# First MoE: the low part of the activations subtracted on VectorE instead of GpSimd

## The chip, the cores and the metric

The kernel runs on one core of a Trainium2 chip. The core has a matmul engine (TensorE, PE in the rows), three engines for elementwise work (VectorE or DVE, ScalarE or ACT, GpSimd or POOL) and an engine that only starts transfers (SyncE, SP). Each runs its own queue of instructions in order, and semaphores tie the queues together. The metric is device time of one execution in microseconds; before the change it is 1246.03 us (median of three runs, 1245.34 to 1246.07).

## What is computed

Attention over 4 batches, 12 heads, 448 positions and 64 columns a head (with an RMS norm on q and k), then two layers of experts over the 1792 tokens. The change is in the first of them, which is one dense expert:

```python
def _moe_ref(x, w_in, w_out):           # x 1792x768, w_in 768x2048, w_out 2048x768
    h = x @ w_in
    g = np.maximum(0.01 * h, h)
    return (g @ w_out).astype(np.float32)
```

The second layer routes each token to one of 8 experts by the largest logit, and so needs the first layer's output to nearly full float32 precision.

## The kernel before

**Products in three parts.** TensorE gets its operands rounded (`fp32r`). To keep the precision, each operand is kept as a high part (rounded copy, by ScalarE) and a low part (the operand less its high part), and each product is the sum of three matmuls: high x high, high x low, low x high. The helper `lo_of(engine, dst, src, hi)` issues the subtraction that makes a low part, as one `tensor_tensor` on the engine it is given. All low parts in the profile stand under its line, L63.

**The first MoE** goes through the 2048 inner columns in 16 blocks `f` of 128, two at a time (a group `G`), and through the four batches `b` of 448 tokens. A unit of `first(f, b)` adds 18 matmuls (6 blocks of the model's 768 columns, times 3; L627 to L629) in a PSUM bank `mo`. ScalarE makes `g` = 0.01 of it, VectorE the larger of the two, ScalarE the high part `gh`, and another engine the low part `gl` (L636; the line that changes). There is one buffer for `g` (so a unit's `g` cannot be made before the `gl` of the unit before), four for `gh` and for `gl`, two banks `mo`. A tile of `second(G, d, b)` is 6 matmuls (2 blocks times 3; L646 to L648) in a PSUM bank `mp` (two banks), which VectorE adds to `ysum` (L654; in the first group ScalarE copies, L652). A group has 8 units and 24 tiles.

**The weights** arrive as 8-byte numbers and are decoded on the way: each half of a block goes through ScalarE's `mag` (L580), five steps on VectorE (`top` L581 to L583, `pw` L585, `raw` L586) and an addition on GpSimd (L588). The buffers of `top`, `pw` and `mag` are single, so a half's first step waits for the addition of the half before. Then ScalarE makes the high part (`w0h` or `w1h`, L596) and GpSimd the low part (`w0l` or `w1l`), called a split here. There are three buffers for `raw` and three of each split weight.

**What sets the order.** The program is written unit by unit, but within the first MoE a scheduler places the instructions of each engine's queue by its own estimate of times. So a change of one instruction's engine changes the order on all engines from there on. DMAs of the weights are in SP's queue.

Of the kernel before, what the change touches and what calls it, by code (L numbers as in the profile page):

```python
# [20 lines left out]
def attention_moe_moe2(  # L21
# [15 lines left out]
    nc = tc.nc  # L37
# [24 lines left out]
    def lo_of(engine, dst, src, hi):  # L62
        engine.tensor_tensor(dst, src, hi.bitcast(F32), ALU.subtract)  # L63
# [87 lines left out]
    def xT_of(b, c):  # L151
        return [t[:, b % 2, c] for t in xT[b // 2]]
# [463 lines left out]
    class FirstMoe:  # L616
# [4 lines left out]
        def first(self, f, b):  # L621
            hi, lo = self.w.done[0, f]
            wh_, wl_ = hi.rearrange("p (c f) -> p c f", c=KD), lo.rearrange("p (c f) -> p c f", c=KD)
            ph = self.p1.tile([P, S], F32, name="mo", bufs=2)
            for c in range(KD):
                xh, xl = xT_of(b, c)
                nc.tensor.matmul(ph, wh_[:, c], xh, start=(c == 0), stop=False)  # L627
                nc.tensor.matmul(ph, wh_[:, c], xl, start=False, stop=False)  # L628
                nc.tensor.matmul(ph, wl_[:, c], xh, start=False, stop=(c == KD - 1))  # L629
            g = self.mw.tile([P, S], F32, name="g", bufs=1)  # L630
            gh = self.mw.tile([P, S], F32R, name="gh", bufs=2 * GF)
            gl = self.mw.tile([P, S], F32R, name="gl", bufs=2 * GF)
            nc.scalar.activation(g, ph, AF.Copy, scale=0.01)
            nc.vector.tensor_tensor(g, ph, g, ALU.max)  # L634
            nc.scalar.activation(gh, g, AF.Copy)  # L635
            lo_of(nc.gpsimd, gl, g, gh)  # L636
            self.gs[f, b] = (gh, gl)
            self.w.use(0, f)

# [472 lines left out]
```

## Time and profile before

| | before |
|---|---|
| median of the runs | 1246.03 us |
| the profiled execution | 1244.74 us, of which the trace spans 1242.7 |
| TensorE busy | 1161.2 us (93%) |
| VectorE busy | 761.7 us (61%) |
| ScalarE busy | 497.6 us (40%) |
| GpSimd busy | 529.5 us (43%) |
| `gl` on GpSimd | 64 instructions, 76.8 us |

The first MoE lies between about 366 and 880 us; attention before it, the second MoE after it. A row of the trace reads: start and duration in us, engine, line, operation, output and inputs, and in square brackets how long the engine stood idle just before and what ended that. `x2` merges two in a row. A VectorE instruction that is held up by another engine's use of the memory counts as busy all the while, so its duration in the row shows it.

### The profile page before, as it was taken

Reading aid. Unit: us, or ns where it says so; the run is one execution under the profiler, and the core shown is the slowest. Engines: PE = TensorE matmul, PEld = TensorE weight load, DVE = VectorE, ACT = ScalarE, POOL = GpSimd, SP = SyncE. Lnnn points to the kernel's source line nnn. Section 1 sums busy time; section 2 is a strip of 40 time slices with the busy share of each in tenths; the row PEclk is TensorE's granted clock in tenths of the full one; section 3 lists DMA queues with packets and bytes.
Section 4 is the critical chain, followed back from the end, with each engine's and each line's share of the span. In section 5 each row is a group of like instructions: output and inputs, shape, how many; then the busy total and the mean of one; then the engine's idle time right before and its main releaser. Section 6 shows DMA issues by size and latency. Waiting matters only on the chain.

```text
span 1242.7 us, 19106 instructions
## 1 busy us (share of the span) xinstructions
PE 1161.2 (93%) x6988; PEld 931.5 (75%) x6988; DVE 761.7 (61%) x1262; ACT 497.6 (40%) x791; POOL 529.5 (43%) x365
## 2 busy tenths in 40 slices
PE   4899999988999899999999999999799999999997
PEld 2455555544668778888888888978588988988986
DVE  6777888866527884757575754346646169315446
ACT  2566666645335421222222322123335257324444
POOL 1567767756445541525252523110325046213334
PEclk9899999989899999999999999999799999999999
DMA  5212222110102220111111110153366049413556
GB/s 147 59 47 64 72 70 73 49 29 29 46 15 76 77 78 23 55 48 53 50 53 49 53 51 1 49 175 96 79 249 246 17 169 358 176 47 109 181 202 224
DMA packets 68081, 116.28 MB, mean 94 GB/s; under 512 B 6780, under 2 KB 45948, under 8 KB 67968
## 3 DMA queue, kind: packets, MB, share of 16 engines
q1 hardware_dynamic: 64528, 103.87, 26.1%
q0 software_dynamic: 3120, 11.02, 2.6%
q8 instruction: 57, 0.93, 0.3%
q14 instruction: 56, 0.46, 0.1%
q10 hardware_dynamic: 320, 0.00, 0.0%
HBM read 106.61 MB, written 12.58 MB: 96 GB/s over the span
## 4 chain that ended last, share of the span: by engine, by line
PE 65%; DVE 16%; issue 7%; POOL 5%; ACT 3%; DMA 3%; ACTq 0%; DVEq 0%; POOLq 0%; SPq 0%
PE sc L298 6%; PE av L309 6%; PE mp L646 4%; PE mo L627 4%; PE mo L628 4%; PE mo L629 4%; PE mp L647 4%; PE mp L648 4%; PE ph L990 4%; PE ph L988 3%; PE ph L989 3%; DVE top L583 3%; PE py L1006 3%; PE py L1004 3%; PE py L1005 3%
## 5 line engine op out<-in xcount | busy, mean ns | idle before, releaser
L654 DVE TENSOR_TENSOR ysum<-mp,ysum 128x448 f32<-128x448 f32 x168 | 103.8, 621 | 113.0 <-PE mp L648 111.8
L313 POOL TENSOR_TENSOR pr<-pr,p 112x896 f32<-112x896 f32 x72 | 152.8, 2122 | 40.5 <-ACT p L300 26.5
L646 PE MATMUL mp<-gh,w1h 128*128 128x448 f32 x384 | 145.8, 381 | 19.9 <-DVE ysum L654 16.5
L627 PE MATMUL mo<-xTh,w0h 128*128 128x448 f32 x384 | 142.2, 370 | 7.0 <-DVE g L634 3.4
L647 PE MATMUL mp<-gl,w1h 128*128 128x448 f32 x384 | 142.4, 371 | 0.0
L628 PE MATMUL mo<-xTl,w0h 128*128 128x448 f32 x384 | 141.9, 369 | 0.2 <-DVE xTl L63 0.2
L629 PE MATMUL mo<-xTh,w0l 128*128 128x448 f32 x384 | 141.3, 368 | 0.0
L648 PE MATMUL mp<-gh,w1l 128*128 128x448 f32 x384 | 140.8, 370 | 0.0
L63 POOL TENSOR_TENSOR gl<-g,gh 128x448 fp32r<-128x448 f32 x64 | 76.8, 1201 | 139.9 <-ACT gh L635 113.2
L588 POOL TENSOR_TENSOR raw<-raw,top 128x384 f32<-128x384 f32 x64 | 64.7, 1012 | 139.2 <-DVE raw L586 114.8
L277 DVE TENSOR_REDUCE md<-tp 112x2 f32<-112x896 f32 x96 | 104.5, 1089 | 18.2 <-PE tp L275 18.0
L1004 PE MATMUL py<-w2h,hT 128*128 128x384 f32 x288 | 99.7, 346 | 0.0
L646 PEld LDWEIGHTS mp<-gh,w1h 128*128 128x128 f32 x384 | 72.8, 190 | 35.4 <-DVE ysum L654 13.8
L1006 PE MATMUL py<-w2l,hT 128*128 128x384 f32 x288 | 96.8, 336 | 0.0
L1005 PE MATMUL py<-w2h,hL 128*128 128x384 f32 x288 | 96.5, 335 | 0.0
L990 PE MATMUL ph<-w1l,xgh 128*128 128x512 f32 x216 | 86.3, 400 | 4.2 <-DVE w1l L63 4.2
L63 DVE TENSOR_TENSOR hL<-pt,hT 128x512 fp32r<-128x512 f32 x36 | 24.8, 689 | 106.2 <-ACTq L1014 59.3
L988 PE MATMUL ph<-w1h,xgh 128*128 128x512 f32 x216 | 86.8, 402 | 0.0
L989 PE MATMUL ph<-w1h,xgl 128*128 128x512 f32 x216 | 85.6, 396 | 0.0
L627 PEld LDWEIGHTS mo<-xTh,w0h 128*128 128x128 f32 x384 | 72.4, 189 | 15.9 <-DVE g L634 3.7
L580 ACT ACTIVATE mag<-wd 128x384 f32<-128x384 f32 x64 | 35.5, 555 | 118.5 <-DVE top L583 57.8
L63 POOL TENSOR_TENSOR w1l<-r,w1h 128x1024 fp32r<-128x1024 f32 x17 | 42.9, 2529 | 93.0 <-ACT w1h L952 75.1
(199 smaller groups left out, 2542.3 us busy)
## 6 DMA issues: line engine op xcount, KB each, us to landing
r<-in_moe_w_dram SPq DMA_DIRECT2D x27, 1024.0 KB, 6.5
r<-in_moe_w_dram SPq DMA_DIRECT2D x36, 768.0 KB, 7.3
wd<-in_moe_w_in_dram SPq DMA_DIRECT2D x32, 384.0 KB, 3.2
wd<-in_moe_w_out_dram SPq DMA_DIRECT2D x32, 384.0 KB
qk<-in_q_dram SPq DMA_DIRECT2D x24, 224.0 KB, 2.8
qk<-in_k_dram SPq DMA_DIRECT2D x24, 224.0 KB, 3.1
vv<-in_v_dram SPq DMA_DIRECT2D x24, 224.0 KB, 2.7
x2d<-xn SPq DMA_DIRECT2D x24, 224.0 KB, 2.9
```

Of the source, the lines that this page charges most:

```text
L63: engine.tensor_tensor(dst, src, hi.bitcast(F32), ALU.subtract)
L313: nc.gpsimd.tensor_tensor(st["pr"][:CP], st["pr"][:CP], p, ALU.add)
L627: nc.tensor.matmul(ph, wh_[:, c], xh, start=(c == 0), stop=False)
L628: nc.tensor.matmul(ph, wh_[:, c], xl, start=False, stop=False)
L629: nc.tensor.matmul(ph, wl_[:, c], xh, start=False, stop=(c == KD - 1))
L646: nc.tensor.matmul(py, hi[:, sl], gh, start=(j == 0), stop=False)
L647: nc.tensor.matmul(py, hi[:, sl], gl, start=False, stop=False)
L648: nc.tensor.matmul(py, lo[:, sl], gh, start=False, stop=(j == GF - 1))
L990: nc.tensor.matmul(ph[n], xh[:, c], w1l[:, c, s_], start=False, stop=(c == K1 - 1))
L1004: nc.tensor.matmul(py[n], hT[:, c], w2h[:, c, s_], start=(c == 0), stop=False)
L1005: nc.tensor.matmul(py[n], hL[:, c], w2h[:, c, s_], start=False, stop=False)
L1006: nc.tensor.matmul(py[n], hT[:, c], w2l[:, c, s_], start=False, stop=(c == K2 - 1))
```

## The change

One word: `gl` is made on VectorE.

```diff
@@ -633,7 +633,7 @@
             nc.scalar.activation(g, ph, AF.Copy, scale=0.01)
             nc.vector.tensor_tensor(g, ph, g, ALU.max)
             nc.scalar.activation(gh, g, AF.Copy)
-            lo_of(nc.gpsimd, gl, g, gh)
+            lo_of(nc.vector, gl, g, gh)
             self.gs[f, b] = (gh, gl)
             self.w.use(0, f)
```

The scheduler orders the queues anew. First, VectorE's queue at the start of a group of weights (the same rows come once in each group; `raw` is the step that waits for the split). Before:

```order
L654 TENSOR_TENSOR ysum<-mp,ysum 128x448 x3
L586 SCALAR_TENSOR_TENSOR raw<-wd,pw 128x384
L654 TENSOR_TENSOR ysum<-mp,ysum 128x448 x2
L634 TENSOR_TENSOR g<-mo,g 128x448
L654 TENSOR_TENSOR ysum<-mp,ysum 128x448 x2
```

After:

```order
L654 TENSOR_TENSOR ysum<-mp,ysum 128x448 x3
L63 TENSOR_TENSOR gl<-g,gh 128x448
L634 TENSOR_TENSOR g<-mo,g 128x448
L586 SCALAR_TENSOR_TENSOR raw<-wd,pw 128x384
L654 TENSOR_TENSOR ysum<-mp,ysum 128x448 x2
L63 TENSOR_TENSOR gl<-g,gh 128x448
L581 TENSOR_SCALAR top<-wd 128x384
```

`gl` and the `g` that depends on it now stand ahead of `raw`. Second, TensorE's queue at the same place, the end of the group's second `mp` tile (the waits are on VectorE and on GpSimd, by their semaphores). Before:

```order
L648 MATMUL mp<-gh,w1l 128x448 [waits Pool_49]
L648 MATMUL mp<-gh,w1l 128x448
L646 MATMUL mp<-gh,w1h 128x448 [waits DVE_49]
L647 MATMUL mp<-gl,w1h 128x448
L648 MATMUL mp<-gh,w1l 128x448
```

After:

```order
L648 MATMUL mp<-gh,w1l 128x448 [waits Pool_49]
L648 MATMUL mp<-gh,w1l 128x448
L627 MATMUL mo<-xTh_114,w0h 128x448 [waits DVE_49]
L628 MATMUL mo<-xTl_115,w0h 128x448
L629 MATMUL mo<-xTh_114,w0l 128x448
```

A whole unit of `mo` has moved ahead of the third tile. Further on in the group five `mp` tiles now follow each other in the midst of a decode. Third, VectorE's queue in that run of five tiles, after:

```order
L581 TENSOR_SCALAR top<-wd 128x384
L654 TENSOR_TENSOR ysum<-mp,ysum 128x448
L582 SCALAR_TENSOR_TENSOR top<-wd,top 128x384
L654 TENSOR_TENSOR ysum<-mp,ysum 128x448
L63 TENSOR_TENSOR gl<-g,gh 128x448
L583 SCALAR_TENSOR_TENSOR top<-mag,top 128x384
L654 TENSOR_TENSOR ysum<-mp,ysum 128x448
L585 TENSOR_SCALAR pw<-top 128x384
L634 TENSOR_TENSOR g<-mo,g 128x448
L654 TENSOR_TENSOR ysum<-mp,ysum 128x448
L586 SCALAR_TENSOR_TENSOR raw<-wd,pw 128x384
```

The decode's steps, a `gl` and a `g` now lie between the five tiles' `ysum`. Fourth, VectorE's queue at the start of the second group of weights (the stretch around 416 us before). Before:

```order
L586 SCALAR_TENSOR_TENSOR raw<-wd,pw 128x384
L581 TENSOR_SCALAR top<-wd 128x384
L634 TENSOR_TENSOR g<-mo,g 128x448
L582 SCALAR_TENSOR_TENSOR top<-wd,top 128x384
L583 SCALAR_TENSOR_TENSOR top<-mag,top 128x384
```

After:

```order
L586 SCALAR_TENSOR_TENSOR raw<-wd,pw 128x384
L634 TENSOR_TENSOR g<-mo,g 128x448
L63 TENSOR_TENSOR gl<-g,gh 128x448
L581 TENSOR_SCALAR top<-wd 128x384
L582 SCALAR_TENSOR_TENSOR top<-wd,top 128x384
```

This `g` has moved ahead of the decode's first step. GpSimd's queue keeps its splits and additions in the order they had in each group; only the rows of `gl` between them are gone.

## Rows read from the trace of the kernel before

**Rows 1.** The head of the page: span, busy time of each engine, instructions.
```profile
span 1242.7 us, 19106 instructions
PE 1161.2 (93%) x6988; PEld 931.5 (75%) x6988; DVE 761.7 (61%) x1262; ACT 497.6 (40%) x791; POOL 529.5 (43%) x365
```

**Rows 2.** Two stretches: length, then busy us of PE, PEld, DVE, ACT, POOL.
```profile
440.00:480.00 40.00, 35.63 (x165) 31.26 (x164) 30.67 (x51) 9.52 (x17) 14.45 (x12) 0.96 0.24 69
...
540.00:600.00 60.00, 57.40 (x279) 51.64 (x278) 39.76 (x69) 16.17 (x28) 24.68 (x20) 1.00 0.16 47
```

**Rows 3.** Groups of instructions: busy us, mean ns of one, idle before and releaser.
```profile
L654 DVE TENSOR_TENSOR ysum<-mp,ysum 128x448 f32<-128x448 f32 x168 | 103.8, 621 | 113.0 <-PE mp L648 111.8
...
L63 POOL TENSOR_TENSOR gl<-g,gh 128x448 fp32r<-128x448 f32 x64 | 76.8, 1201 | 139.9 <-ACT gh L635 113.2
```

**Rows 4.** Splits on VectorE in the second MoE: duration ns least/median/most.
```profile
L63 DVE TENSOR_TENSOR w1l<-r,w1h x31: 1216/1227/3436, 900.3 to 1216.4; 128x1024 fp32r<-128x1024 f32 x31
...
L63 DVE TENSOR_TENSOR w2l<-r,w2h x48: 942/946/2321, 905.4 to 1228.0; 128x768 fp32r<-128x768 f32 x48
```

**Rows 5.** Waits: who for whom, us in total, times, the longest.
```profile
ACT g L633 <- POOL gl L63: 59.7, 42, 2.6
...
PE mp L646 <- DVE ysum L654: 16.5, 13, 2.1
```

**Rows 6.** In order of time around 561 us (stall A), and its last repetition.
```profile
559.52 1.85 POOL L63 TENSOR_TENSOR w1l<-raw,w1h 128x768 fp32r<-128x768 f32 x1 [10.35 <-ACT w1h L596]
...
561.33 1.15 POOL L63 TENSOR_TENSOR gl<-g,gh 128x448 fp32r<-128x448 f32 x1
561.41 1.49 DVE L586 SCALAR_TENSOR_TENSOR raw<-wd,pw 128x384 f32<-128x384 uint32 x1 [1.35 <-POOL w1l L63]
...
561.49 0.60 PE L648 MATMUL mp<-gh,w1l 128*128 128x448 f32 x2
562.43 2.15 POOL L63 TENSOR_TENSOR w1l<-raw,w1h 128x768 fp32r<-128x768 f32 x1
...
563.48 0.47 PE L646 MATMUL mp<-gh,w1h 128*128 128x448 f32 x1 [1.39 <-DVE ysum L654]
...
750.43 0.47 PE L646 MATMUL mp<-gh,w1h 128*128 128x448 f32 x1 [1.39 <-DVE ysum L654]
```

**Rows 7.** In order of time from 584 to 592 us (stall B).
```profile
584.48 0.37 PE L627 MATMUL mo<-xTh,w0h 128*128 128x448 f32 x1
...
584.92 1.83 POOL L63 TENSOR_TENSOR w0l<-raw,w0h 128x768 fp32r<-128x768 f32 x1 [0.96 <-ACT w0h L596]
585.41 1.77 DVE L583 SCALAR_TENSOR_TENSOR top<-mag,top 128x384 f32<-128x384 f32 x1
...
589.70 0.36 DVE L581 TENSOR_SCALAR top<-wd 128x384 int32<-128x384 int32 x1 [1.12 <-POOL raw L588]
...
590.43 0.36 PE L629 MATMUL mo<-xTh,w0l 128*128 128x448 f32 x1
590.76 0.56 DVE L583 SCALAR_TENSOR_TENSOR top<-mag,top 128x384 f32<-128x384 f32 x1
591.23 0.62 DVE L654 TENSOR_TENSOR ysum<-mp,ysum 128x448 f32<-128x448 f32 x1
...
592.00 0.44 PE L646 MATMUL mp<-gh,w1h 128*128 128x448 f32 x1 [1.21 <-DVE ysum L654]
```

**Rows 8.** In order of time between 380 and 470 us, five rows.
```profile
382.19 1.51 DVE L583 SCALAR_TENSOR_TENSOR top<-mag,top 128x384 f32<-128x384 f32 x1
...
416.46 1.94 DVE L581 TENSOR_SCALAR top<-wd 128x384 int32<-128x384 int32 x1 [1.11 <-POOL raw L588]
416.50 0.54 ACT L633 ACTIVATE g<-mo 128x448 f32<-128x448 f32 x1
...
418.99 0.47 PE L627 MATMUL mo<-xTh,w0h 128*128 128x448 f32 x1 [3.36 <-DVE g L634]
...
465.24 1.29 DVE L581 TENSOR_SCALAR top<-wd 128x384 int32<-128x384 int32 x1 [0.64 <-POOL raw L588]
```

## Prediction

> **What bounds the kernel now.** I read the page's head first, then the stages, the stalls of the first MoE one by one, and last the queue orders of both kernels. TensorE is busy for 1161.2 of 1242.7 us, VectorE for 761.7, GpSimd for 529.5 [rows 1]: on average GpSimd, which the change relieves, is far from a bound. The average hides the stage, so the second view is the table of stretches: from 440 to 480 us TensorE works 35.63 of 40 us with VectorE at 30.67, from 540 to 600 us 57.40 of 60 with VectorE at 39.76 and GpSimd at 24.68 [rows 2]. What can be won is what TensorE waits, about a tenth in the first of these stretches and a twentieth in the second.
>
> The change touches 64 instructions of 1.20 us on GpSimd [rows 3]. They feed `gl`, and two things hang on them: the next `g`, since there is one buffer for it (ScalarE waited 59.7 us for `gl`, in 42 cases), and, through VectorE's queue, TensorE: it waits for `ysum`, which empties the two `mp` banks, 16.5 us in 13 cases [rows 5]. So I followed the waits for `ysum` in order of time. From 501 us on they repeat with each group of weights, every 62.3 us (563.48 to 750.43 is three periods): a wait of 1.39 us (stall A, at 563.48; five such in all) and one of 1.21 us (stall B, at 592.00; four in all) [rows 6, 7]. Matmuls start every 0.205 us (30 from 584.48 to 590.43 [rows 7]). So the one due after the pair that starts at 561.49 was due at 561.90, and A costs 563.48 - 561.90 = 1.58 us; B costs 592.00 - 590.64 = 1.36 us.
>
> What makes them: in A VectorE's `raw` waits until GpSimd's split `w1l` ends (559.52 + 1.85 = 561.37), and then takes 1.49 us, because `gl` runs on GpSimd from 561.33 to 562.48; `ysum` is queued behind it. In B the split `w0l` (584.92 to 586.75) holds `top` for 1.77 us, and `ysum`, queued behind the next decode's first step, comes at 591.23. The same steps of the decode with nothing beside them take 0.56 us (line 583) and 0.36 (line 581) [rows 7]; so these steps do not run while GpSimd works, and one that was waiting goes ahead of GpSimd's next operation: the `w1l` at 562.43 took 2.15 us where the one before took 1.85 [rows 6]. `gl`, with two inputs in SBUF like `raw`, I count as such a step; `ysum`, with one in PSUM, is not (mean 0.621 over 168 [rows 3]).
>
> **What the change costs and gives.** On GpSimd 64 x 1.20 = 76.8 us go; nothing waits less for that in itself, since splits and additions are released by ScalarE, TensorE and VectorE. On VectorE 64 subtractions come. No row shows this form there, so it is bounded: splits of two SBUF inputs take 0.942 us for 768 columns and 1.216 for 1024 at the least [rows 4], 1.07 ns a column, hence 0.942 - 320 x 0.00107 = 0.60 us for 448; `ysum`, of the same shape with one input in PSUM, takes 0.62 [rows 3]. From above, one that waits for a split: 0.60 + 1.85 = 2.45 us (the worst split on VectorE took 3.436 against 1.216, 2.2 us of waiting [rows 4]). From below, nothing at all where VectorE would have stood waiting anyway. I take 0.60 and count each collision where the order puts one. Behind a `gl` that waits for ScalarE's `gh` now stand `ysum`, `g` and the decode on VectorE; for them wait TensorE's `mp` and `mo` banks.
>
> *Start, 366 to 470 us.* Here the decode fills VectorE. In 11 places a decode step beside a `gl` takes 0.8 to 0.95 us longer (the first 1.51 instead of 0.56 at 382.19, the last 1.29 instead of 0.36 at 465.24 [rows 7, 8]): 11 x 0.86 = 9.4 us go. In the same stretch 12 subtractions of 0.60 come: 7.2 us. That leaves 2.2 us on a chain that TensorE sees here. The largest single wait, 3.36 us at 418.99, is for a `g` whose ScalarE half ended at 417.04 and which stood in the queue behind a `top` held by a split (416.46 + 1.94 = 418.40) [rows 8]; in the new order this `g` stands ahead of that `top`, and starts at about 417.1 instead of 418.33 (418.99 less one VectorE step of 0.62 and the handover): 1.2 us. Sum 3.4 us.
>
> *Steady part, stall A.* In the new order TensorE has a unit of `mo` (18 matmuls, 3.7 us) after the second `mp` tile, so `raw` and the `ysum` behind it have time. But this unit needs the bank that `g` frees, and VectorE's queue now reads `ysum` x3, `gl`, `g`, `raw`. `gl` waits for the split to end at 561.37, then 0.60 for itself, 0.54 for ScalarE's `g` [rows 8], 0.62 for VectorE's, and some 0.1 of handovers: 563.23. TensorE wanted to go on at 561.90: 1.33 us against 1.58 now, a gain of 0.25.
>
> *Steady part, stall B.* The old place is harmless in the new order, but TensorE now has five `mp` tiles in a row (30 matmuls, 6.15 us), just when the first `w0l` split runs: it is released by the last matmuls of the unit before. The split holds the decode step ahead of `ysum` for its 1.85 us; by counting steps the third tile of the run starts 1.4 us late and the fifth 0.3 more: 1.7 us against 1.36 now, a loss of some 0.3. Five times A and four times B cancel (-1.25 and +1.4): 0, +- 1 us.
>
> *Tail, from 780 us.* No decode is left, VectorE has room; the routing's chain at the end holds only one `gl`. Nothing, +- 1 us. DMAs keep their queue, SP's, and their places.
>
> Sum: 1244.74 us (the profiled execution) - 3.4 = 1241.3. The median of the runs, 1246.03, lies 1.3 above the profiled one; against it I expect 1242.6 us.
>
> The rule that speaks most against the change stands in the Trainium skill, "SBUF — State Buffer", section "Who interferes with whom": a VectorE instruction with two SBUF inputs collides with a GpSimd instruction that reads SBUF, and whichever issues first has the shared ports to its end. The 1.49 us beside `gl` agree [rows 6]; but of who is next when both wait the page says only that the order of issue decides, while the row of 2.15 us shows VectorE first. By the page alone GpSimd's second split could as well go first in A, which is the second rival below.
>
> **Rivals.**
> 1. *The gain at the start is hidden.* The decode is paced by its own loop (a decode step waits for the addition, as 1.12 us at 589.70 [rows 7]) and by the splits, which stay; then the 2.2 us are not seen and only the 1.2 us of one `g` are left, or not even these: 1245 us. For it: the largest excesses in rows 7 and 8, 1.2 to 1.6 us, belong to splits, not to `gl`. Against it: 11 places with `gl` in 90 us.
> 2. *Slower: in A the second split takes the port ahead of `gl`.* Its ScalarE half is ready in time, so GpSimd starts it at 561.37 and `gl` waits 1.85 us more, `g` and the whole `mo` unit with it: 3.2 us instead of 1.6, five times 1.6 = 8 us, less the 3.4 of the start: 1250.6 us. It decides when `gl` reaches VectorE's head after 561.37 (a late `gh`, behind two splits on ScalarE) or if the port is not given to the one who waits. Against it: the 2.15 us.
> 3. *Better than forecast.* The split in B comes a step later than I count and falls beside `ysum`, which it does not hold, or into the next `mo` unit. B goes (1.36 x 4 = 5.4 us) and A keeps its 0.25 x 5 = 1.25: 1246.03 - 3.4 - 6.7 = 1236 us. It needs VectorE to be ahead of my count by about one step, 0.6 us.
> 4. *The change doesn't do what it says.* In the new order GpSimd has only splits and additions in this stage; excluded.
>
> **How the numbers follow.** Forecast 0.40 (1238 to 1246 by itself), rival 1 0.23, rival 2 0.22, rival 3 0.15. No change means within 0.2% (2.5 us), which is about what a measurement of this kernel can tell. The forecast is faster in three of four cases, else the same; rival 1 is the same in 0.18 and slower in 0.05; rival 2 slower in 0.20; rival 3 faster. Faster 0.30 + 0.15 = 0.45, same 0.30, slower 0.25. The range reaches from rival 3 to rival 2, a little more on each side: 1235 to 1252 us.
>
> **What would show it.** In the trace after: (1) `gl` on VectorE, 0.6 us at its least and up to 2.4; (2) the wait at the first `mo` unit after the start of a group of weights, released by `g`, about 1.3 us, in place of A's for `ysum`: 3 us there is rival 2; (3) one or two waits for `ysum` within a run of five `mp` tiles, 1.7 us together, beside a `w0l` split: none there is rival 3; (4) the wait near 419 us down from 3.36 to about 2.1; (5) no decode step between 366 and 470 us stretched by 0.8 to 0.95 us, only by splits and by additions. I am wrong if the period is not 62.3 +- 1 us, or if new waits for `g` stand where none is now, `gl` holding VectorE while `gh` is late.

## The result and the profile after

The changed kernel took 1231.39 us (median of four runs, 1230.19 to 1232.06) against 1245.76 us beside it: a ratio of 0.9884 (0.9868 to 0.9900), 14.4 us faster. Forecast were 1242.6 us in a range from 1235 to 1252: the direction is right, the gain is four times the forecast one (3.4 us).

The head of the page after, to be read against [rows 1]; columns as there:

```profile
span 1228.4 us, 19094 instructions
...
PE 1158.2 (94%) x6988; PEld 930.8 (76%) x6988; DVE 775.5 (63%) x1326; ACT 500.3 (41%) x791; POOL 456.4 (37%) x301
```

GpSimd lost 73.1 us, VectorE gained only 13.8, though 64 subtractions came to it. The stretches of [rows 2], after (the third number from the end is the share of TensorE's clock that was granted, then come the share of the DMA engines and GB/s):

```profile
440.00:480.00 40.00, 39.64 (x192) 35.46 (x191) 31.15 (x58) 11.00 (x19) 9.80 (x8) 1.00 0.21 59
...
540.00:600.00 60.00, 59.05 (x285) 53.04 (x285) 43.37 (x80) 16.46 (x28) 15.99 (x12) 1.00 0.19 53
```

TensorE works 4.0 us more of the first 40 us and 1.65 more of the later 60: it waits for almost nothing there. The first stretch also differs in the granted clock, 0.96 in [rows 2] and 1.00 here. Before, TensorE waited for `ysum` three times between 459 and 468 us (0.74, 2.11 and 1.52 us), and from 467.16 to 470.57 us the clock was at the lower of its two levels (0.50, that is 1.2 of 2.4 GHz). Two of these waits, and matmuls at the lower and again at the full clock, before:

```profile
464.75 0.44 PE L646 MATMUL mp<-gh,w1h 128*128 128x448 f32 x1 [2.11 <-DVE ysum L654]
...
467.72 0.74 PE L646 MATMUL mp<-gh,w1h 128*128 128x448 f32 x1 [1.52 <-DVE ysum L654]
...
468.63 0.58 PE L648 MATMUL mp<-gh,w1l 128*128 128x448 f32 x1
469.00 0.58 PE L646 MATMUL mp<-gh,w1h 128*128 128x448 f32 x1
...
470.95 0.36 PE L646 MATMUL mp<-gh,w1h 128*128 128x448 f32 x1
471.15 0.37 PE L647 MATMUL mp<-gl,w1h 128*128 128x448 f32 x1
```

Matmuls start every 0.375 us there, and every 0.205 us at the full clock. In the changed kernel the waits are gone, and so is this stretch.

Rows of instructions after, for [rows 3]; then the durations of `gl` (least/median/most); then ScalarE's waits, for [rows 5]:

```profile
L654 DVE TENSOR_TENSOR ysum<-mp,ysum 128x448 f32<-128x448 f32 x168 | 103.8, 621 | 111.1 <-PE mp L648 109.5
...
L646 PE MATMUL mp<-gh,w1h 128*128 128x448 f32 x384 | 144.4, 377 | 1.4 <-ACT ysum L652 0.7
```

```profile
L63 DVE TENSOR_TENSOR gl<-g,gh x64: 607/617/1904, 330.5 to 849.0; 128x448 fp32r<-128x448 f32 x64
```

```profile
ACT g L633 <- DVE gl L63: 55.6, 44, 2.0
```

`ysum` is as long as before. TensorE's 16.5 us of waits for it are gone: all idle time ahead of these `mp` matmuls is 1.4 us; ScalarE waits for `gl` about as long as before, on another engine.

Where the 14.4 us came from is read by the first matmul of each group of `mp` tiles, after less before, on the two profiled executions (1152 such matmuls in each, in their order): -0.8 us at the first group, -3.9 at the second, -9.3 at the third, then about -1.5 a group to -15.2 at the seventh and -15.7 at the eighth; 1.5 us are given back from there to the end of the span. So some 8.5 us belong to the first two groups, and the steady period fell from 62.3 to 60.8 us (552.13 to 612.99 below is 60.86).

In the first two groups (128.9 us long before, 120.4 after) TensorE's idle time fell from 11.2 to 5.2 us: waits for VectorE's `ysum` from 4.4 to 0, for ScalarE's copy (L652) from 3.4 to 0.7, for `g` up from 3.4 to 4.1. Of its matmuls there 26 started at the lower clock before and 18 after, which by the two spacings above is 8 x 0.17 = 1.4 us. The remaining 1.2 us I did not place.

The start of a steady group after, the place of stall A [rows 6]; in order of time:

```profile
548.51 4.00 POOL L63 TENSOR_TENSOR w1l<-raw,w1h 128x768 fp32r<-128x768 f32 x2 [16.81 <-ACT w1h L596]
...
548.95 1.89 DVE L63 TENSOR_TENSOR gl<-g,gh 128x448 fp32r<-128x448 f32 x1
...
550.68 0.57 PE L648 MATMUL mp<-gh,w1l 128*128 128x448 f32 x2
...
550.88 0.54 ACT L633 ACTIVATE g<-mo 128x448 f32<-128x448 f32 x1 [1.24 <-DVE gl L63]
...
551.46 0.62 DVE L634 TENSOR_TENSOR g<-mo,g 128x448 f32<-128x448 f32 x1 [0.61 <-ACT g L633]
552.00 0.94 DVE L586 SCALAR_TENSOR_TENSOR raw<-wd,pw 128x384 f32<-128x384 uint32 x1
...
552.13 0.47 PE L627 MATMUL mo<-xTh,w0h 128*128 128x448 f32 x1 [0.88 <-DVE g L634]
...
612.99 0.47 PE L627 MATMUL mo<-xTh,w0h 128*128 128x448 f32 x1 [0.89 <-DVE g L634]
```

This is the forecast chain: `gl` stands behind the first split, goes ahead of the second, then ScalarE's `g`, VectorE's `g`, TensorE. Ten microseconds on, the first `w0l` split, where a wait of 1.7 us was forecast (stall B's successor):

```profile
562.92 0.36 DVE L581 TENSOR_SCALAR top<-wd 128x384 int32<-128x384 int32 x1 [1.19 <-POOL raw L588]
...
562.99 1.99 POOL L63 TENSOR_TENSOR w0l<-raw,w0h 128x768 fp32r<-128x768 f32 x1
...
563.51 0.62 DVE L654 TENSOR_TENSOR ysum<-mp,ysum 128x448 f32<-128x448 f32 x1 [0.23 <-PE mp L648]
...
564.05 1.35 DVE L582 SCALAR_TENSOR_TENSOR top<-wd,top 128x384 int32<-128x384 int32 x1
...
565.33 0.61 DVE L654 TENSOR_TENSOR ysum<-mp,ysum 128x448 f32<-128x448 f32 x1
...
565.99 0.19 PEld L646 LDWEIGHTS mp<-gh,w1h 128*128 128x128 f32 x1 [0.42 <-DVE ysum L654]
```

The decode step `top` slipped in 0.07 us ahead of the split, `ysum` ran through beside it (its `mp` is in PSUM), and only the next decode step was held, until 565.40; what is left on TensorE is 0.42 us in the weight load; the matmul behind it starts 0.20 us late. And the end of the first group, the wait of [rows 8]:

```profile
411.20 1.91 POOL L63 TENSOR_TENSOR w1l<-raw,w1h 128x768 fp32r<-128x768 f32 x1 [0.74 <-ACT w1h L596]
...
411.50 0.54 ACT L633 ACTIVATE g<-mo 128x448 f32<-128x448 f32 x1
...
411.55 1.97 DVE L583 SCALAR_TENSOR_TENSOR top<-mag,top 128x384 f32<-128x384 f32 x1
...
414.43 0.62 DVE L634 TENSOR_TENSOR g<-mo,g 128x448 f32<-128x448 f32 x1
...
415.10 0.69 PE L627 MATMUL mo<-xTh,w0h 128*128 128x448 f32 x1 [4.08 <-DVE g L634]
```

This wait grew, from 3.36 to 4.08 us: `g` now stands behind the last three steps of a decode half, the first of them held by a split.

### The profile page after: what moved, and what is told of

Same layout as the page of the kernel before. It is cut to its first block, busy times and chain, and to the rows that moved or that the text cites. A ratio compares the mean times of both kernels' runs of the same rounds, so it can differ in the third digit from the quotient of the medians.

```text
span 1228.4 us, 19094 instructions
## 1 busy us (share of the span) xinstructions
PE 1158.2 (94%) x6988; PEld 930.8 (76%) x6988; DVE 775.5 (63%) x1326; ACT 500.3 (41%) x791; POOL 456.4 (37%) x301
## 4 chain that ended last, share of the span: by engine, by line
PE 77%; DVE 10%; issue 5%; ACT 3%; DMA 2%; POOL 2%; ACTq 0%; DVEq 0%; POOLq 0%; SPq 0%
PE mo L627 6%; PE mo L628 6%; PE mo L629 6%; PE sc L298 6%; PE av L309 6%; PE mp L646 6%; PE mp L647 5%; PE mp L648 5%; PE ph L990 4%; PE ph L989 3%; PE ph L988 3%; PE py L1006 3%; PE py L1004 3%; PE py L1005 3%; DVE w1l L63 2%
## 5 line engine op out<-in xcount | busy, mean ns | idle before, releaser
L277 DVE TENSOR_REDUCE md<-tp 112x2 f32<-112x896 f32 x96 | 104.4, 1088 | 17.7 <-PE tp L275 17.4
L627 PEld LDWEIGHTS mo<-xTh,w0h 128*128 128x128 f32 x384 | 72.5, 189 | 24.1 <-DVE g L634 12.1
L63 POOL TENSOR_TENSOR w1l<-raw,w1h 128x768 fp32r<-128x768 f32 x16 | 31.4, 1984 | 141.7 <-ACT w1h L596 141.7
L300 ACT ACTIVATE p<-sc 112x896 f32<-112x896 f32 x72 | 66.0, 917 | 39.8 <-PE sc L298 35.6
```

## The experiments

Four accounts were set against each other. **Port**: a VectorE step with its operands in SBUF stands while GpSimd reads SBUF, so GpSimd's `gl` cost time on VectorE. **Queue**: GpSimd's own time and the places in its queue were what the change freed. **Chain**: the way from `g` over `gl` to the next `g` became shorter. **Order**: the scheduler's new order alone did it. "Decode steps" are lines 581 to 586 on VectorE. Ratios are to the kernel before, run beside each.

**1. Give GpSimd reads back** (the results of the added work are not used):

```diff
             lo_of(nc.vector, gl, g, gh)
+            if f < NF - GF:
+                for t in (tab, stab):
+                    nc.gpsimd.tensor_tensor(t, gh[:NTAB, :P].bitcast(F32), gh[:NTAB, :P].bitcast(F32), ALU.subtract)
```

> The kernel after, with dummy work put back on GpSimd where gl was: in the 56 units of the first seven groups two subtractions of 112x128, which wait for gh, read it twice and write zeros into two small tables that hold zeros until the last group. The order of the other queues stays nearly as after (TensorE: 63 of 6582 instructions stand elsewhere, all in the steady part). About 0.48 us each by the slope of GpSimd's splits, 54 us in all against gl's 77. Theory P (while GpSimd reads SBUF, VectorE's decode steps stand still): two thirds of the gain is lost again, 1239 to 1243 us. Theory Q (gl delayed the additions and splits in GpSimd's queue): 1235 to 1238. Theory C (the shorter way from g over gl to the next g) and theory O (the new order of the queues alone): 1231 to 1233.

1238.58 us, ratio 0.9939 (0.9915 to 0.9963): nearly half of the gain is gone and the period is back at about 62.0 us. The time lies between the numbers of the port theory (from 1239) and of the queue theory (to 1238), and the interval holds both. The rows show little of the loss as a step held by a dummy. One place: a dummy now stands between the two `w1l` splits, so the second begins later and meets more of `raw`:

```profile
493.95 1.83 POOL L63 TENSOR_TENSOR w1l<-raw,w1h 128x768 fp32r<-128x768 f32 x1
...
494.53 1.67 DVE L586 SCALAR_TENSOR_TENSOR raw<-wd,pw 128x384 f32<-128x384 uint32 x1
```

In the changed kernel this second split had half a microsecond left when `raw` came (0.94 us); here it had 1.25 (1.67). But no wait of TensorE follows from it. The wait that grew comes from the order: 63 of the 6988 matmuls in the trace changed places, and the last `mo` matmul on a `w0l` buffer is one of them (experiment 3).

**2. The same with fills, which read nothing** (four `memset` of 112x128 a unit on GpSimd, nothing else changed).

> As e1_reads, but the dummy work reads nothing: four memsets of 112x128 a unit on GpSimd, behind no wait but their own queue; the order of the instructions on TensorE, VectorE and ScalarE is that of the kernel after, instruction for instruction. Theory P: 1231 to 1233, as the kernel after, since nothing is read. Theory Q: as far back as e1_reads, some 1235 to 1238. Theories C and O: 1231 to 1233.

1243.04 us, ratio 0.9977 (0.9967 to 0.9987), but it tells nothing of the port: with no input, the fills of both tiles all ran within the first 55 us of the program. One tile's:

```profile
L639 POOL MEMSET tab<- x112: 194/199/229, 2.6 to 50.7; 112x128 f32 x112
```

The first matmul behind the attention then came 12.87 us later (378.84 against 365.97), and the period stayed at 60.8 us. 44.5 us of GpSimd, put at the start of the program, cost 13.

**3. Fills tied to their unit** by a copy of one column on ScalarE.

```diff
+            if f < NF - GF:
+                nc.scalar.activation(tab[:, :1], gh[:NTAB, :1].bitcast(F32), AF.Copy)
+                for _ in range(5):
+                    nc.gpsimd.memset(tab, 0.0)
```

> The changed kernel plus, per unit of all groups but the last, five GpSimd fills of 112x128 that read nothing (199 ns each by the run before, so about 1.0 us a unit, as much of GpSimd's time as the two dummy subtractions took, 1.08 us), tied to the unit by a one-column ScalarE copy so that they stand in the first MoE. Port theory (GpSimd's reads of SBUF hold VectorE): no reads are added, so it stays near the changed kernel, 1231 to 1234 us, period 60.8 us. Queue theory (GpSimd's time itself is what was freed): as with the dummy subtractions, 1237 to 1240 us, period near 62.0 us.

1235.74 us, ratio 0.9917 (0.9900 to 0.9935): between the two theories, so neither number held. In order of time at the place of the new wait:

```profile
567.03 0.37 PE L629 MATMUL mo<-xTh,w0l 128*128 128x448 f32 x1
...
567.55 1.84 POOL L63 TENSOR_TENSOR w0l<-raw,w0h 128x768 fp32r<-128x768 f32 x1 [1.58 <-ACT tab L638]
...
567.93 1.94 DVE L63 TENSOR_TENSOR gl<-g,gh 128x448 fp32r<-128x448 f32 x1
...
569.32 0.73 POOL L640 MEMSET tab<- 112x128 f32 x3
...
569.79 0.54 DVE L583 SCALAR_TENSOR_TENSOR top<-mag,top 128x384 f32<-128x384 f32 x1
```

The fills hold nothing: `top` takes its 0.54 us beside them, and of 91 such VectorE steps beside nothing but fills none took over 0.11 us longer than unheld. What moved is the `w0l` split. It waits for the last `mo` matmul that reads its buffer, which the new order (93 of the 6988 matmuls changed places) puts behind two `mp` tiles: it ends at 567.40, 2.7 us after the rest of its unit (the row names ScalarE's copy, which ends at the same time). So the split catches `gl`, which takes 1.94 us, and TensorE has a new wait of 1.05 us a group; the period grows by 0.7 us, to 61.6. Experiment 1 has the same late matmul, and 0.97 us of the same wait, which is most of the 1.2 us by which its period grew. Neither run is a clean measure of the port. The Trainium skill, "SBUF — State Buffer", section "Who interferes with whom", says that a VectorE instruction with two SBUF inputs collides with a GpSimd instruction that reads SBUF and not with one that only writes; the last row here agrees.

**4. A written order**: the first MoE's loop issued in program order, once with `gl` on GpSimd, once on VectorE, with the same order on TensorE and ScalarE.

> The kernel before, but from the end of attention on the first MoE's queues are in the order in which the program is written, not the scheduler's; gl on GpSimd. The base for e8_manual_vector. It will be slower than before, since decode and units are not interleaved: 1260 to 1300 us by all theories.

> As e7_manual_gpsimd with gl on VectorE: TensorE's and ScalarE's queues have the same order in both, VectorE's has only the 64 subtractions more. Theories P and C: faster than e7_manual_gpsimd by 6 to 14 us, most of the gain without any new order. Theory O: within 3 us of e7_manual_gpsimd, or slower.

1455.41 us (1.1671, 1.1648 to 1.1695) and 1483.45 us (1.1895, 1.1871 to 1.1919): here the same move is 28 us **slower**, where both port and chain had it faster; the order account alone allowed that. The base missed its expectation too, by over 150 us: TensorE ran at the lower clock for 291 us in the one and 299 in the other, against 58 in the kernel before. What TensorE waits for in the two, `gl` on GpSimd first:

```profile
PE mp L646 <- DVE ysum L654: 128.3, 10, 14.0
```

```profile
PE mp L646 <- DVE ysum L654: 151.8, 26, 15.7
```

I read this as sums that stand at the end of VectorE's queue: 64 x 0.626 = 40 us more in the queue come out as 23.5 us more of wait for `ysum`, with all 6988 matmuls in the same order. So added VectorE work has a price, and it depends on what is queued behind it.

**5. The change for the first two groups alone, and for the others alone** (`nc.vector if f < 2 * GF else nc.gpsimd`, and the reverse).

> The low part of g on VectorE for the first two groups alone, on GpSimd after. If the gain is local to where the subtraction stands (port), the first 9.3 us of the 14.4 remain and the 1.5 us per period do not: about 1236.5 us, first stretch as in the changed kernel, period near 62.3 us. If the gain comes from one new order of the queues that spans the stage, the steady period could stay near 60.8 us and the time near 1231 us, or the whole gain go, 1243 us or more.

> The complement: GpSimd for the first two groups, VectorE after. Port theory: only the 1.5 us a period of the steady groups, some 4 to 6 us in all: about 1240 to 1242 us, with the stalls of 390, 411 and 459 to 468 us back. If the two halves don't add up (this run's gain and that of the first two groups together well under or over 14.4 us), the order of the queues has a part of its own.

1236.06 us (0.9926, 0.9906 to 0.9946) and 1241.09 us (0.9954, 0.9936 to 0.9971), both as expected: -10.0 and -4.9, together -14.9 against -14.4 for the whole. The gain is local to where the subtraction stands. A single new order that spans the stage is excluded; small ones, as in experiment 3, are not, since each of the two runs has the new order where it has the change.

**6. `g` in PSUM**: `max` written back to `ph`, and `gh` and `gl` made from it.

```diff
-            nc.vector.tensor_tensor(g, ph, g, ALU.max)
-            nc.scalar.activation(gh, g, AF.Copy)
-            lo_of(nc.vector, gl, g, gh)
+            nc.vector.tensor_tensor(ph, ph, g, ALU.max)
+            nc.scalar.activation(gh, ph, AF.Copy)
+            lo_of(nc.vector, gl, ph, gh)
```

> The changed kernel with max(ph, g) written back into PSUM and both parts of g made from there, so that the one SBUF buffer of g is free after the max and the VectorE subtraction has one operand in SBUF. If the 0.88 us per period and most of the 4.08 us at 415 us are the wait for that buffer, they go: 1224 to 1228 us. Rival: the PSUM buffer of mo is then held through the subtraction instead (two of them), or PSUM reads make the step slower than 0.62 us: 1231 to 1236 us.

1233.24 us, ratio 0.9901 (0.9883 to 0.9918): no gain on the change, but for neither reason of the rival.

```profile
L63 DVE TENSOR_TENSOR gl<-mo,gh x64: 608/615/628, 331.2 to 851.5; 128x448 fp32r<-128x448 f32 x64
```

```profile
580.73 0.44 PE L646 MATMUL mp<-gh,w1h 128*128 128x448 f32 x1 [1.27 <-DVE ysum L654]
```

With one input in PSUM, `gl` was not held once in 64 (most 0.628 us, against 1.904 with both in SBUF). The 0.88 us for `g` are gone, and the split holds the decode step behind it instead (line 582 0.85 us in the mean from 480 to 780 us, 0.65 in the changed kernel): 1.27 us for `ysum`. The period is the same, and the first two groups took 3.7 us longer than in the changed kernel. So a `gl` that nothing held went with no gain here.

**7. Splits or additions on VectorE too** (the changed kernel, `lo_of(nc.vector, lo, raw, hi)` in the split for both weights; for `w1` alone; and, apart, the decode's addition on VectorE).

> The changed kernel with the low halves of the first MoE's weights made on VectorE as well, so that GpSimd has the decode's additions alone. Port theory: what still holds VectorE in the changed kernel are GpSimd's splits of 1.85 to 2 us (29 of them, 55 us); on VectorE they take about 0.94 us each, 27 us, and the held time that goes is about (824 - 617) ns x 51 for the subtraction of g, 10.5 us, and some 15 us of decode steps. The 4 us at 415 us and the 0.88 us a period go or halve: 1222 to 1229 us. Queue theory: 27 us more in VectorE's queue, in front of sums that TensorE waits for, at no gain for GpSimd, which had time: 1232 to 1240 us.

> As the run before, but only the splits of the second weight (w1) are on VectorE: these are the ones behind which the subtraction of g waits once a period (0.88 us) and behind which a decode step stands at 411 us. Port theory: the 0.88 us and most of the 4.08 us go, the splits of w0 go on holding VectorE: 1224 to 1230 us. Queue theory: 1231 to 1236 us.

> The changed kernel with the decode's additions on VectorE too (0.56 us by the other steps of that shape, against 1.01 us on GpSimd), so that GpSimd has the splits alone. Port theory: the additions fall where VectorE waits for them anyway, so they hold little; the splits, which hold, stay: 1229 to 1233 us, no gain worth the name. Rival: the decode's chain of eight steps loses an engine change and 0.45 us an addition and so catches up: 1222 to 1228 us.

Both weights: **1226.04 us**, ratio 0.9846 (0.9824 to 0.9868), as the port theory had it, and the lowest time here. The gain over the change lies in the first two groups (114.9 us long against 120.4): the 4.08 us halved to 2.11, and the clock fell only once there (9 matmuls at the lower level). In the steady groups 1.31 us for `ysum` took the place of the 0.88, and the period is 60.7 us. `w1` alone: 1232.66 us (0.9896, 0.9880 to 0.9913), no gain, as the queue theory had it and not the port theory: the 4.08 us halved to 2.12, but 1.11 us a group for `ysum` took the place of the 0.88. Additions: 1261.06 us (1.0130, 1.0113 to 1.0147), which neither account had. Most of the loss lies ahead of the steady groups: the first matmul behind the attention comes at 390.32 us instead of 365.97, which is 24.4 of the 29.8 us between the two traces. Ten of these additions fall into the attention, where GpSimd reads for over 2 us at a time:

```profile
L588 DVE TENSOR_TENSOR raw<-raw,top 128x384 f32<-128x384 f32 x10 | 18.0, 1799 | 0.3
```

Seven of the ten took 2.31 to 2.34 us and three 0.56; those in the first MoE (54 from 366 to 780 us) have a mean of 0.64. Behind each of the seven stands `md` (L277), for which TensorE then waits 2.4 us in six cases. The first:

```profile
138.95 2.33 DVE L588 TENSOR_TENSOR raw<-raw,top 128x384 f32<-128x384 f32 x1
...
142.34 0.46 PE L275 MATMUL tp<-kh,qh 64*112 64x448 f32 x2 [2.42 <-DVE md L277]
```

After each of these six waits TensorE's granted clock fell to the lower level (0.50) for 3.4 or 6.8 us; from 55 to 366 us its mean is 0.94, against 0.98 in the changed kernel.

**8. The splits moved instead of `gl`** (the kernel before with `lo_of(nc.vector, lo, raw, hi)` alone).

> The kernel before, with the low part of g left on GpSimd and the weights' splits on VectorE instead: the other half of the last version without the change itself. Unheld, the five VectorE steps of a decode half take 2.375 us (555+557+552+356+355 ns), 125.9 us for 53; they took 172.6 us in the kernel before, 142.7 us in the changed one, so 46.7 us were held of which the subtraction of g on GpSimd had 29.9 us. Port theory: those 29.9 us stay, some 17 us go, and 27 us of splits are added to VectorE: 1238 to 1244 us, decode steps about 155 us in all. If either move alone were enough (a GpSimd relieved by 55 us, as by the change), about 1231 us.

1228.62 us, ratio 0.9862 (0.9840 to 0.9885). My expectation, 1238 to 1244, was wrong: either move alone gives most of what both give. The decode steps took 150.5 us, near the 155 expected; so the term that fails is the 27 us of splits that I added as a cost.

The four kernels side by side, from 366 to 480 us (length, then busy us of PE, PEld, DVE, ACT, POOL): before, changed, splits moved instead, both moved.

```profile
366.00:480.00 114.00, 101.89 (x461) 88.81 (x462) 86.78 (x133) 43.23 (x80) 53.66 (x42) 0.96 0.25 73
```

```profile
366.00:480.00 114.00, 108.66 (x507) 96.80 (x508) 85.76 (x150) 45.65 (x83) 39.86 (x30) 0.97 0.26 73
```

```profile
366.00:480.00 114.00, 109.72 (x515) 98.48 (x516) 85.47 (x149) 46.56 (x84) 37.48 (x34) 0.97 0.26 73
```

```profile
366.00:480.00 114.00, 109.71 (x526) 99.76 (x527) 86.83 (x165) 46.44 (x85) 20.28 (x20) 0.99 0.25 73
```

VectorE is busy for the same 86 us in all four, with 133 to 165 instructions in them; TensorE gains 7 to 8. What differs in VectorE's rows is how much of that time is standing. Two of the decode's steps from 366 to 780 us show it (busy us, mean ns | idle before), in the same order:

```profile
L583 DVE SCALAR_TENSOR_TENSOR top<-mag,top 128x384 f32<-128x384 f32 x53 | 45.0, 850 | 2.8
L582 DVE SCALAR_TENSOR_TENSOR top<-wd,top 128x384 int32<-128x384 int32 x53 | 40.7, 768 | 1.5
```

```profile
L583 DVE SCALAR_TENSOR_TENSOR top<-mag,top 128x384 f32<-128x384 f32 x53 | 33.0, 623 | 2.4
...
L582 DVE SCALAR_TENSOR_TENSOR top<-wd,top 128x384 int32<-128x384 int32 x53 | 32.7, 618 | 1.4
```

```profile
L582 DVE SCALAR_TENSOR_TENSOR top<-wd,top 128x384 int32<-128x384 int32 x53 | 33.0, 622 | 1.4
...
L583 DVE SCALAR_TENSOR_TENSOR top<-mag,top 128x384 f32<-128x384 f32 x53 | 32.2, 607 | 2.0
```

```profile
L582 DVE SCALAR_TENSOR_TENSOR top<-wd,top 128x384 int32<-128x384 int32 x53 | 29.5, 557 | 1.4
L583 DVE SCALAR_TENSOR_TENSOR top<-mag,top 128x384 f32<-128x384 f32 x53 | 29.3, 552 | 0.9
```

With both moved the steps are at their unheld length, though GpSimd still makes 54 additions of 1.01 us there: VectorE's next decode step mostly waits for them anyway. All five steps together took 172.6, 142.7, 150.5 and 126.5 us. With what was moved to VectorE (`gl` 42.2; splits 18.6 + 15.6; both 35.6 + 14.6 + 13.6) its work in the stretch went from 172.6 to 184.9, 184.7 and 190.3 us: **VectorE's work rose each time, and the kernel became faster each time.** The order changed each time as well (against the kernel before, 1071, 1072 and 642 of the 6988 matmuls stand elsewhere), so this is no clean measure of held time either.

## Why the prediction was wrong

**The start, 366 to 470 us: the step that failed.** I took 9.4 us of held decode steps off and put 7.2 us of subtractions on, as if both stood in one chain that TensorE sees, and kept 2.2 us. This term was mis-sized: the first two groups gave 8.5 us on the trace although the wait at 419 us grew, and 10.0 us in the run that had the change in them alone. The holds went much as forecast: the trace has ten decode steps stretched by a `gl` (8.7 us; I had counted eleven), and adding up what each SBUF-only step of VectorE took over its unheld length in the first two groups, 23.3 us before and 11.9 after, holds on `gl` itself included. The subtractions came as forecast too, but none of TensorE's waits there hangs on a `gl`: VectorE is busy for 86 of these 114 us, and else waits for GpSimd's addition (13.0 us in 15 waits) and for matmuls. That they cost nothing there is argued from this, not measured; in experiment 4 they had a price. The last experiment shows the same error from the other side: 34 us of splits on VectorE, entered as a cost, went with a kernel 16.9 us faster.

What the sum lacked is TensorE's own waits, which I listed for the steady part and, but for one, not for the start: 11.2 us before, 5.2 after. They do not pair off with the steps beside `gl`. The 1.42 us at 411.71 and the 0.74 at 459.92 hang on decode steps held by a split (at 408.53 and 455.77), the 2.11 at 464.75 on a decode's steps one after the other, the 1.52 at 467.72 on a step held by `gl` (465.24 [rows 8]). So it is in part luck that the 8.5 us lie near the 8.7 of held steps. The clock was put at nothing without a reason, though [rows 2] shows 0.96: 1.4 us. Rival 1, that this gain is hidden by the decode's own pace, is refuted by the run with the change in these two groups alone.

**The wait at 419 us.** Forecast 2.1 us, measured 4.08 [rows 8]: I placed `g` ahead of the next `top` and did not see three steps of the decode before it, one held. The gain of 1.2 us was a loss of 0.7.

**Stall A: mechanism right.** `gl` took VectorE's turn ahead of the second split, as the 2.15 us row suggested [rows 6], and rival 2 fell. TensorE was due at 550.68 + 2 x 0.205 = 551.09 and started at 552.13: 1.04 us lost against 1.33 forecast and 1.58 before.

**Stall B: rival 3.** I counted the split ahead of `top`; it came 0.07 us behind. Forecast 1.7 us, measured two matmuls 0.20 us late. (Before, `ysum` stood behind three steps of the next decode, not behind its first alone as I wrote.) So A and B did not cancel: 0.54 + 1.36 = 1.9 us less of the two stalls, of which 1.5 us a period are seen; the rest went into those two. This second term, forecast at 0 ± 1 us in all, gave some 6 us by the eighth group, and by my own sign (a period of 62.3 ± 1 us) the prediction was wrong there too. Rival 3 had its place and condition right, at a chance of 0.15, and by itself with my start it gave 1236 us.

**The tail**, forecast 0 ± 1: 1.5 us lost.

**(5), no step stretched by `gl` or its like from 366 to 470 us**: right; the steps still stretched there stand beside splits, which now hold `gl` itself in places (1.13 us long at 391.34).

What stays open is how the 14.4 us divide between the steps that GpSimd's `gl` held and the places of splits and matmuls that the new order moved. Both exist. Experiments 1 and 3 were to divide them and gave back some 7 and 4 us, but both also moved a matmul on TensorE, and the third has a ScalarE copy in each unit and a first MoE that began 1.6 us later; so no share is put on either. That TensorE pays for held time, and not for VectorE's own work, is argued from experiments 6 to 8 and not shown: they change the order too, and the held time in sum does not rank the kernels. From 366 to 780 us VectorE's steps are held for 46.6 us before, 25.8 in the changed kernel, 42.5 in experiment 1, 27.0 with `g` in PSUM, 15.0 with the `w1` splits moved too, 3.7 with all splits moved too and 31.8 with the splits moved instead. The gains of the last six over the kernel before are, in that order, 14.4, 7.9, 12.8, 12.1, 18.7 and 16.9 us.

## What to carry to other kernels

Where VectorE and GpSimd work side by side on SBUF, do not add busy times: list each GpSimd instruction that reads SBUF and look at which VectorE step stands at the head of the queue when it begins, and what is behind that step. Then list TensorE's own waits in that stretch, and the clock it was granted after them: these are what a move can win. Moving such an instruction to VectorE made the kernel 14.4 us faster in the scheduler's order and 28 us slower in the written one. Try the long readers too: here the splits of 1.85 to 2 us, moved alone, gave 16.9 us, about as much as the 64 shorter subtractions (14.4; the intervals of the two overlap), and both together 18.7, far from the sum.

## What the runs showed of the hardware

- One operand in PSUM is enough to run beside GpSimd's reads: `gl` with `mo` in PSUM took 0.608 to 0.628 us in 64 of 64 cases, 0.607 to 1.904 with both operands in SBUF; `ysum` stayed at 0.62 us in every run.
- A step with a single operand in SBUF was held too: line 581, 0.36 us by itself, took 1.94 us beside a split [rows 8].
- Five GpSimd fills of 112x128 (0.20 us each) beside VectorE's decode held no step, while seven additions on VectorE took 2.31 to 2.34 us for 0.56 where GpSimd's 2.1 us reads of the attention ran beside them.
- TensorE's granted clock fell to the lower level (0.50) during the third of three waits (0.74, 2.11 and 1.52 us, from 459 to 468 us in the kernel before) and after each of six waits of 2.42 us in the attention of the additions run; matmuls of 128x448 started every 0.375 us in the first of these stretches, 0.205 outside.
